# Talking-heads attention with a gated feed-forward network: the network's first product in float32 under the next batch's attention, x kept on chip, second head mixing on quarters of the array, 45 tiles a batch, w_out decoded late

## The chip, the cores and the metric

One core of a Trainium2 chip runs one program. The time is the device time of one execution in microseconds; the span of a profile runs from its first to its last instruction.

## The reference

For each of 4 batches: 12 heads, 448 rows, 64 elements a head. Scores are mixed over heads before and after the softmax; the result, 448 x 768, goes through a network with a convolution of three taps along the rows as its gate.

```python
scores = scale * q @ k^T                     # b h i j
scores = einsum('bhij,hg->bgij', scores, w_pre)
attn   = softmax(scores over j)              # sum + 1e-9
attn   = einsum('bhij,hg->bgij', attn, w_post)
x      = (attn @ v) as [b, 448, 768]
h      = relu(x @ w_in)                      # 768 -> 1024
gate   = sigmoid(conv_w[0]*h[i-1] + conv_w[1]*h[i] + conv_w[2]*h[i+1])
out    = (h * gate) @ w_out                  # 1024 -> 768
```

`w_in`, `conv_w` and `w_out` come as 64-bit floats and are decoded to float32 on the chip.

## The kernel before, in words

The rows of a batch are cut into four chunks of 120, 120, 120 and 100 query rows (`CHUNKS`, line 22), and a chunk into tiles of ten rows: 46 tiles a batch, 184 in all. A chunk goes through these steps, each a function:

- `qk` (line 372): scores of two heads (tile s), 64 x 64 quarters of the array; `qk_out` copies them, `relayout` (line 401) brings each head's scores by one DMA into a tile mt whose partitions hold ten rows of twelve heads.
- `premix` (line 411): two tiles at a time, mt times block-diagonal `wpre`, on quarters, into tiles m. `row_max`, `row_exp` (line 427), `sum_eps`, `sum_rec`, `post_w` make exponentials e and, for each tile, the second mixing's weights divided by the row sums (wn).
- `postmix` (line 451): for each tile four products, 124 partitions of e as weights, 112 columns of them, 120 columns of wn, on the whole array; the zeros of block-diagonal wn are multiplied too. `post_out` (line 462) copies the tile t on ScalarE.
- `av` (line 477): eight products a head pair on two halves of the array, into tile a of the pool ps_a (one buffer); `av_out` copies, `x_out` stores x (tensor xT) to DRAM.

A product of float32 operands appears as two records of TensorE in the trace (`postmix`: eight a tile).

The weights are decoded in 48 pieces of 256 KB (`dec_load`, `dec_step`, line 517 on): 24 of `w_in`, split into a high and a low part in reduced float32 (F32R), 24 of `w_out`, stored to DRAM. After all attention the network runs batch by batch: `x_load` and a split, `mm1` (line 625; three products of parts for each of six slices of 128, for each of eight slices f of the 1024), `relu`, `conv`, `gate`, `glu`, the split of g, and `mm2` (line 680) for 14 groups of 128 rows.

The order of instructions on each engine is planned ahead: `Order` (line 47) takes operations with a due time, an engine, a cost and the operations they wait for, and emits them in the order in which they could start. All DMAs of the main part are issued by SyncE (SP), in order, and each waits until the eighth DMA before it has landed; a DMA whose data is not ready holds those behind it.

Of the kernel before, what the change touches and what calls it, by code (L numbers as in the profile page):

```python
# [8 lines left out]
F32 = mybir.dt.float32  # L9
# [24 lines left out]

LAG = {"PE": P["lpe"], "DVE": P["ldve"], "ACT": P["lact"], "POOL": P["lpool"], "SP": P["lsp"]}

CUT = {"premix": 4, "qk": 4, "av": 2}
TURN = .093  # L40


RELAY = ("SP", (.82, .57))


class Order:

# [5 lines left out]
    def add(self, due, engine, cost, fn, *args, after=(), since=0.0):  # L53
        key = (fn.__name__, *args)
        assert key not in self.ops, key
        self.ops[key] = (due, len(self.ops), engine, cost, fn, args, tuple(after), since)

    def run(self, free, look):
        waits, users, ready = {}, {}, {e: [] for e in free}
        for key, op in self.ops.items():  # L60
            missing = {k for k in op[6] if k in self.ops}
            waits[key] = len(missing)
            for k in missing:
                users.setdefault(k, []).append(key)

        def release(key):
            due, i, engine, cost, fn, args, after, since = self.ops[key]
            t = since
            for k in after:
                if k in self.done:  # L70
                    end, e = self.done[k]
                    t = max(t, end + (LAG[e] if e != engine or e in ("SP", "DVE") else 0))
            ready[engine].append((due, i, t, key))
# [4 lines left out]
        left = len(self.ops)  # L78
        wire = 11.6
        cut = 1  # L80
        while left:
            best = None
            for e, ops in ready.items():
                if ops:
                    t0 = min(max(free[e], o[2]) for o in ops)
                    o = min(o for o in ops if o[2] <= max(t0, free[e]) + look)
# [6 lines left out]
            due, i, engine, cost, fn, args, after, since = self.ops[o[3]]  # L93
            if e == "PE":
                new = CUT.get(o[3][0], 1)
                if new != cut:
                    cost += TURN if new > 1 else 2 * TURN
                cut = new
            if isinstance(cost, tuple):
                cost, move = cost  # L100
                wire = max(wire, t + cost + .65) + move
                self.done[o[3]] = wire, "SP"
            else:
                self.done[o[3]] = t + cost, e
            free[e] = t + cost
            fn(*args)
            left -= 1
            for k in users.get(o[3], ()):
                waits[k] -= 1
                if waits[k] == 0:  # L110
                    release(k)


@with_exitstack
def tile_talking_heads_conv_glu(
# [13 lines left out]
    B, H, S, D = q.shape  # L129
    DM, FF = w_in.shape  # L130
    NP = H // 2
    NIB = S // 32
    JC = 4
    JW = S // JC
    scale = 1.0 / float(D) ** 0.5
    KC = DM // 128
    FC = FF // 128

    dram = ctx.enter_context(tc.tile_pool(name="dram", bufs=1, space=DRAM))

    xT = [dram.tile([128, NP * S], F32, name=f"xT{b}") for b in range(B)]

    w_out_s = dram.tile([FF, DM], F32, name="w_out_s")
# [18 lines left out]
    tasks = []  # L162

    def at(time, fn, *args):
        tasks.append((time, len(tasks), fn, args))

    def run(some):
        for _, _, fn, args in sorted(some, key=lambda e: (e[0], e[1])):
            fn(*args)

    if True:
        def pool(name, bufs, **kw):
            return ctx.enter_context(tc.tile_pool(name=name, bufs=bufs, **kw))

        const = pool("const", 1)
        ko_p = pool("ko", 7)
        qo_p = pool("qo", 2)
        nk_p = pool("nk", 2)
        nq_p = pool("nq", 1)
        wi_p = pool("wi", 1)  # L180
        mt_p = pool("mt", 2)
        st_p = pool("st", 3)
        e_p = pool("e", 4)
        sm_p = pool("sm", 4)
        wn_p = pool("wn", 3)
        at_p = pool("at", 2)
        v_p = pool("v", 6)
        x_p = pool("x", 2)
        dr_p = pool("dr", 3)
        dw_p = pool("dw", 2)  # L190
        ps_q = pool("ps_q", 2, space=PSUM)
        ps_m = pool("ps_m", 3, space=PSUM)
        ps_t = pool("ps_t", 2, space=PSUM)
        ps_a = pool("ps_a", 1, space=PSUM)

        wpre = const.tile([128, 2, 64], F32, name="wpre")
        wpost = const.tile([128, 12, HR, 2], F32, name="wpost")
        cws = const.tile([128, 3, FC], U32, name="cws")

        wraw = const.tile([128, 2, 12], F32, name="wraw")  # L200

        def load_weights():
            nc.gpsimd.memset(wraw, 0.0)
            nc.gpsimd.dma_start(out=wraw[4:124, 0, :],
                                in_=w_pre.rearrange("(o h) g -> o h g", o=1).to_broadcast([2 * HR, 12, 12]))
            for s in range(2):
                nc.gpsimd.dma_start(out=wraw[64 * s:64 * s + 12 * HR, 1, :],
                                    in_=w_post.rearrange("(o h) g -> o h g", o=1).to_broadcast([HR, 12, 12]))

        def emit_weights():  # L210
            raw = wraw
            pre = wpre[:, :, 0:12 * HR].rearrange("p s (r g) -> p s r g", g=12)
            bd = wn_p.tile([128, 2, HR, 12], F32, tag="wn", name="wbd")
            nc.gpsimd.memset(wpre, 0.0)
            for s in range(2):
                nc.vector.tensor_scalar(
                    out=bd[:, s],
                    in0=raw[:, 0, :].rearrange("p (o g) -> p o g", o=1).to_broadcast([128, HR, 12]),
                    scalar1=scale, scalar2=None, op0=ALU.mult)
                nc.gpsimd.affine_select(out=bd[:, s], in_=bd[:, s], pattern=[[-12, HR], [0, 12]],  # L220
                                        compare_op=ALU.is_ge, fill=0.0, base=-4 - 12 * HR * s, channel_multiplier=1)
                nc.gpsimd.affine_select(out=pre[:, s], in_=bd[:, s], pattern=[[12, HR], [0, 12]],
                                        compare_op=ALU.is_ge, fill=0.0, base=15 + 12 * HR * s, channel_multiplier=-1)
            bd2 = wn_p.tile([128, 12, HR, 2], F32, tag="wn", name="wbd2")
            nc.vector.tensor_copy(
                out=wpost.rearrange("p g r s -> p g (r s)"),
                in_=raw[:, 1, :].rearrange("p (g o) -> p g o", o=1).to_broadcast([128, 12, 2 * HR]))
            nc.gpsimd.affine_select(out=bd2, in_=wpost, pattern=[[0, 12], [-12, HR], [-64, 2]],
                                    compare_op=ALU.is_ge, fill=0.0, base=0, channel_multiplier=1)
            nc.gpsimd.affine_select(out=wpost, in_=bd2, pattern=[[0, 12], [12, HR], [64, 2]],  # L230
                                    compare_op=ALU.is_ge, fill=0.0, base=11, channel_multiplier=-1)

        cwraw = const.tile([128, 3 * FC, 2], U32, name="cwraw")
# [697 lines left out]
```

## Time and profile before

| | us |
|---|---|
| three runs | 734.51, 741.04, 742.68 |
| median | 741.04 |
| span of the profiled execution | 730.1 |
| TensorE busy | 691.4 |
| last exponential of the attention starts | 484.69 |

The profile gives the span of the execution it shows, and no device time of its own; the three runs lie 4.4 to 12.6 us above the span. Names of tiles: s scores, m first mixing, t second mixing, a values, h first product of the network, o its second. PE is TensorE, PEld its weight loads, DVE VectorE, ACT ScalarE, POOL GpSimd, SP SyncE. "64*64" in front of a shape is the rows and columns of the array in use.

### The profile page before, as it was taken

What the parts mean: (1) busy time and instruction counts of PE and PEld (TensorE: products, weight loads), DVE (VectorE), ACT (ScalarE), POOL (GpSimd) and SP (SyncE); (2) the same over time, 40 slices, a digit from 0 to 9 for tenths busy, and PEclk for the clock granted to TensorE, in tenths of its full rate; (3) what the DMA queues carried; (4) which work ended last, traced back from release to release, by engine and by line L of the source; (5) the groups of instructions that cost most, each with busy time, mean ns of one, the idle gap of its engine ahead of it and who ended that gap; (6) DMA issues with size and microseconds to landing.
All of it is one profiled execution on the core that took longest, in us unless ns stands there. A gap on an engine that the chain in (4) does not pass through costs nothing.

```text
span 730.1 us, 16150 instructions
## 1 busy us (share of the span) xinstructions
PE 691.4 (95%) x5804; PEld 525.2 (72%) x5804; DVE 419.0 (57%) x1150; ACT 398.5 (55%) x1011; POOL 98.8 (14%) x253
## 2 busy tenths in 40 slices
PE   4697989989999999999999999999999999999997
PEld 3244646656566666576666677788999999999997
DVE  3364576666687666566665654666825722842830
ACT  1255665867778657677767767773512421431420
POOL 7011212212122221121121100100000000000000
PEclk9888999999999999999999999999999999999999
DMA  6698876688876888967666833632212112110011
GB/s 106 198 163 189 210 187 166 201 212 198 196 211 167 222 217 228 217 183 213 198 173 200 204 116 93 198 107 63 51 44 60 38 44 70 27 52 38 1 40 48
DMA packets 104779, 101.26 MB, mean 139 GB/s; under 512 B 55848, under 2 KB 92028, under 8 KB 104700
## 3 DMA queue, kind: packets, MB, share of 16 engines
q1 hardware_dynamic: 102797, 99.62, 51.8%
q8 instruction: 46, 0.75, 0.5%
q10 hardware_dynamic: 1807, 0.61, 0.4%
q14 instruction: 33, 0.27, 0.1%
q0 software_dynamic: 96, 0.01, 0.0%
HBM read 46.48 MB, written 14.16 MB: 83 GB/s over the span
## 4 chain that ended last, share of the span: by engine, by line
PE 76%; DMA 14%; ACT 3%; DVE 2%; issue 2%; POOL 2%; SPq 1%; ACTq 0%; DVEq 0%; POOLq 0%
PE t L458 16%; PE h L637 16%; PE o L695 16%; PE s L385 9%; PE a L483 9%; PE m L419 8%; DMA mt<-st 7%; DMA raw<-in_moe_w_in_dram 5%; DMA nq<-in_q_dram 2%; ACT e L431 1%; POOL mt L313 1%; ACT st L338 1%; ACT at L466 1%; DVE nm L424 1%; DVE mq L301 1%
## 5 line engine op out<-in xcount | busy, mean ns | idle before, releaser
L458 PEld LDWEIGHTS t<-wn,e 124*112 124x112 f32 x1472 | 161.1, 180 | 61.9 <-PE s L385 19.0
L458 PE MATMUL t<-wn,e 124*112 124x120 f32 x1472 | 179.3, 276 | 3.0 <-ACT at L466 2.9
L338 ACT COPY st<-s 120x448 f32<-120x448 f32 (+1 forms) x180 | 94.0, 544 | 70.9 <-DMA mt<-st 39.6
L385 PE MATMUL s<-mk,mq 64*64 64x448 f32 (+2 forms) x768 | 117.2, 575 | 11.3 <-ACT st L338 8.5
L431 ACT ACTIVATE e<-m,nm 124x448 f32<-124x448 f32 x184 | 119.3, 649 | 10.7 <-DVE nm L424 6.9
L424 DVE TENSOR_REDUCE nm<-m 124x1 f32<-124x448 f32 x184 | 109.7, 613 | 25.0 <-PE m L419 22.2
L419 PE MATMUL m<-mt,wpre 64*64 64x448 f32 (+1 forms) x736 | 113.4, 566 | 8.7 <-ACT e L431 4.0
L466 ACT COPY at<-t 112x480 f32<-112x480 f32 x184 | 105.9, 575 | 26.0 <-PE t L458 25.3
L637 PE MATMUL h<-w,w 128*128 128x448 f32 x576 | 119.0, 367 | 0.0
L637 PEld LDWEIGHTS h<-w,w 128*128 128x128 f32 x576 | 107.8, 188 | 9.1
L695 PE MATMUL o<-wo,ga 128*128 128x384 f32 x504 | 91.9, 336 | 0.0
L695 PEld LDWEIGHTS o<-wo,ga 128*128 128x128 f32 x504 | 88.0, 188 | 0.1
L483 PEld LDWEIGHTS a<-at,v 112*64 112x64 f32 x1536 | 75.5, 137 | 15.8 <-ACT at L466 5.0
L437 POOL TENSOR_SCALAR sm<-sm 124x1 f32<-124x1 f32 x184 | 42.6, 231 | 319.5 <-ACT e L431 315.7
L483 PE MATMUL a<-at,v 112*64 112x120 f32 (+1 forms) x1536 | 83.5, 264 | 0.0
L442 DVE RECIPROCAL rs<-sm 124x1 f32<-124x1 f32 x184 | 29.1, 158 | 69.9 <-POOL sm L437 67.0
L419 PEld LDWEIGHTS m<-mt,wpre 64*64 64x64 f32 (+1 forms) x736 | 32.4, 135 | 49.7 <-ACT e L431 20.1
L641 ACT ACTIVATE hpad<-h 128x448 f32<-128x448 f32 x32 | 17.5, 547 | 90.6 <-PE h L637 71.8
L385 PEld LDWEIGHTS s<-mk,mq 64*64 64x64 f32 (+2 forms) x768 | 27.4, 129 | 48.1 <-ACT st L338 23.6
L448 DVE TENSOR_SCALAR wn<-wpost,rs 124x120 f32<-124x120 f32 x184 | 50.5, 274 | 10.7 <-PE t L458 4.6
L150 POOL TENSOR_SCALAR dw<-dw 128x256 f32<-128x256 f32 x48 | 41.5, 865 | 65.1 <-ACT dw L148 63.9
L706 DVE COPY os<-o 128x384 f32<-128x384 f32 x13 | 7.2, 558 | 71.4 <-PE o L695 71.4
(72 smaller groups left out, 519.4 us busy)
## 6 DMA issues: line engine op xcount, KB each, us to landing
mt<-st SPq DMA_DIRECT2D x144, 210.0 KB
nq<-in_q_dram SPq DMA_DIRECT2D x56, 168.0 KB
mt<-st SPq DMA_DIRECT2D x48, 175.0 KB
nk<-in_k_dram SPq DMA_DIRECT2D x72, 108.0 KB
raw<-in_moe_w_in_dram SPq DMA_DIRECT2D x24, 256.0 KB
raw<-in_moe_w_out_dram SPq DMA_DIRECT2D x24, 256.0 KB
v<-in_v_dram SPq DMA_DIRECT2D x48, 112.0 KB
out_dram<-os SPq DMA_DIRECT2D x13, 384.0 KB
```

The costliest lines, as they stand in the source:

```text
L338: nc.scalar.copy(out=out, in_=in_)
L385: nc.tensor.matmul(out=pqs[c, h - 1 + i][m:e], lhsT=qops[c][s, p, o + m:o + e], rhs=kops[b, p][s], start=True, stop=True)
L419: nc.tensor.matmul(out=pms[c, 2 * k + i][64 * s:64 * s + 64], lhsT=wpre[rows, i], rhs=mts[c][rows, 2 * k + s], start=True, stop=True)
L424: nc.vector.tensor_reduce(out=nm[0:PN], in_=pms[c, t][0:PN], axis=AX.X, op=ALU.max, negate=True)
L431: nc.scalar.activation(out=e[0:PN], in_=pms.pop((c, t))[0:PN], func=AF.Exp, bias=nm[0:PN], accum_out=sm[0:PN])
L437: nc.gpsimd.tensor_scalar(out=sm[0:PN], in0=sm[0:PN], scalar1=1e-9, scalar2=None, op0=ALU.add)
L448: nc.vector.tensor_scalar(out=wn[0:PN], in0=wpost.rearrange("p g r s -> p (g r s)")[0:PN], scalar1=rs[0:PN], scalar2=None, op0=ALU.mult)
L458: nc.tensor.matmul(out=ps[:, j].rearrange("p g r -> p (g r)"), lhsT=e[0:PN, j * JW:(j + 1) * JW], rhs=wn[0:PN], start=True, stop=True)
L466: nc.scalar.copy(out=ats[c][:, :, :, t * R:(t + 1) * R], in_=pts.pop((c, t)))
L483: nc.tensor.matmul(out=pas[c][64 * hh:64 * hh + 64, p % 3, 0:n], lhsT=vts[b, p][:, hh, j, :], rhs=ats[c][:, j, 2 * p + hh, 0:n], start=(j ...
L637: nc.tensor.matmul(out=ps, lhsT=w[:, sl], rhs=x, start=(kk == 0 and i == 0), stop=(kk == KC - 1 and i == 2))
L695: nc.tensor.matmul(out=ps[o], lhsT=g, rhs=w, start=(f == 0 and j == 0), stop=(f == FC - 1 and j == 2))
```

## The change

- The last chunk of a batch has nine tiles: 45 a batch; the odd tile's `premix` is one product on 124 partitions.
- `postmix` works on pairs of tiles. The weights wn lose the block of zeros (60 columns instead of 120); the two halves of e's partitions, and halves of 64 columns of e, go to the four quarters of the array. The results of a pair fill two banks, one for each five rows of every tile; `post_out` copies one on ScalarE and one on VectorE. Sums, reciprocals and `post_w` are done once a pair. v is padded to 512 rows with zeros.
- x of a batch stays in one tile on chip. `mm1` of batch b runs under the attention of batch b+1, in plain float32 without splits, with ps_a for its result; h goes to DRAM (`store_h`) and comes back in the last stage (`load_h`). Batch 3's `mm1` follows the attention.
- `w_in` is decoded into one tile, all 24 pieces by the first `mm1`; `w_out` from tile 106 on.
- The planner's costs and due times are new, and it models sixteen DMA rings and eight outstanding DMAs.

```diff
-CHUNKS = [(10, 12), (10, 12), (10, 12), (10, 10)]
+TILES = (12, 12, 12, 9)
...
+    turns = []
+    for c in range(NCH):
+        if c >= 4:
+            turns += [("mm1", c // 4 - 1, 2 * (c % 4) + i) for i in range(2)]
+        turns += [("av", c, 0), ("av", c, 3)]
...
+    for x, y in zip(order, order[1:]):
+        before[y] = ("relu", *x[1:]) if x[0] == "mm1" else ("av_out", *x[1:])
...
+            for i in range(len(some)):
+                add(n + 1 + P["po"] + .01 * i, "PE", .5, "postmix", *x, i, after=[("post_w", *x)] + (
+                    [("post_out", *prev, s) for s in range(2)] if prev else []))
...
+        ready = [("av_out", 4 * b + 3, p) for p in (0, 3)] + [("dec_step", i, 4) for i in range(N_IN)]
...
+            for kk in range(KC):
+                add(n + d * kk, "PE", .77, "mm1", b, f, kk, after=ready + turn + [("mm1", b, f, kk - 1)])
...
-            ps = ps_t.tile([JW, JC, 12, R], F32, tag="t", name="t")
-            for j in range(JC):
-                nc.tensor.matmul(out=ps[:, j].rearrange("p g r -> p (g r)"), lhsT=e[0:PN, j * JW:(j + 1) * JW],
-                                 rhs=wn[0:PN], start=True, stop=True)
+    if i == 0:
+        pts[c, k] = [ps_t.tile([128, 2, JC, 60], F32, tag="t", name="t") for s in range(2)]
+    e, wn = es.pop((c, 2 * k + i)), wns[c, k]
+    for j in range(JC):
+        for half in range(2):
+            o = min(128 * j + 64 * half, S - 64)
+            for s in range(2):
+                rows = slice(64 * s, 64 * s + 12 * HR)
+                nc.tensor.matmul(out=pts[c, k][s][64 * half:64 * half + 64, i, j], lhsT=e[rows, o:o + 64],
+                                 rhs=wn[rows, i], start=True, stop=True)
...
-            nc.scalar.copy(out=ats[c][:, :, :, t * R:(t + 1) * R], in_=pts.pop((c, t)))
+    copy_of(("ACT", "DVE")[s],
+            ats[c][:, :, :, o:o + 5 * n].rearrange("p j g (i r) -> p i (j g) r", r=HR),
+            pts[c, k][s][:, 0:n].rearrange("p i j (g r) -> p i (j g) r", r=HR))
...
-            for kk in range(k0, k1):
-                sl = slice(kk * 128, (kk + 1) * 128)
-                xh, xl = xp[b, kk]
-                for i, (w, x) in enumerate(((lo, xh), (hi, xh), (hi, xl))):
-                    nc.tensor.matmul(out=ps, lhsT=w[:, sl], rhs=x, start=(kk == 0 and i == 0),
-                                     stop=(kk == KC - 1 and i == 2))
+    if kk == 0:
+        pl, tag = (ps_a, "a") if b + 1 < B else (ps_q, "s")
+        phs[b, f] = pl.tile([128, S], F32, tag=tag, name="h")
+    nc.tensor.matmul(out=phs[b, f], lhsT=wi[:, kk, f * 128:(f + 1) * 128].bitcast(F32), rhs=xs[b][:, kk],
+                     start=(kk == 0), stop=(kk == KC - 1))
...
+def store_h(b, f):
+    nc.sync.dma_start(out=h_s[b][f * 128:(f + 1) * 128, :], in_=hss.pop((b, f)))
...
+def load_h(b, f):
+    nc.sync.dma_start(out=hpad[(FC * b + f) % 3][:, 1:S + 1], in_=h_s[b][f * 128:(f + 1) * 128, :])
```

TensorE in the attention of batch 1, before (s `qk`, m `premix`, t `postmix`, a `av`):

```order
L385 MATMUL s<-mk,mq 64x448 x2
L385 MATMUL s<-mk,mq 56x448 x2
L419 MATMUL m<-mt,wpre 64x448 x4
L458 MATMUL t<-wn,e 112x120 x8
L385 MATMUL s<-mk,mq 64x448 x2
L385 MATMUL s<-mk,mq 56x448 x2
L419 MATMUL m<-mt,wpre 64x448 x4
L483 MATMUL a<-at,v 64x100 x24
```

and in the attention of a later batch of the changed kernel (h is the first product of the batch before, six slices each):

```order
L709 MATMUL a<-at,v 64x120 x24
L624 MATMUL m<-mt,wpre 64x448 x4
L588 MATMUL s<-mk,mq 64x448 x2
L588 MATMUL s<-mk,mq 26x448 x2
L757 MATMUL h<-x,wi 128x448 x6
L668 MATMUL t<-wn,e 64x60 x32
L757 MATMUL h<-x,wi 128x448
L588 MATMUL s<-mk,mq 64x448 x2
L588 MATMUL s<-mk,mq 26x448 x2
L757 MATMUL h<-x,wi 128x448 x2
L624 MATMUL m<-mt,wpre 64x448 x4
L668 MATMUL t<-wn,e 64x60 x32
```

Twelve slices of the network's first product stand in each chunk from batch 1 on, in runs between scores, mixings and values.

SyncE late in batch 0, before (mt relayouts, raw pieces of weights, nk and nq loads of k and q, xT the store of x):

```order
L404 DMA mt<-st 10x10x448 x2
L517 DMA raw<-in_moe_w_in_dram 128x512
L293 DMA nq<-in_q_dram 32x6x224 x4
L507 DMA xT_57<-x 128x720
L404 DMA mt<-st 10x12x448 x4
L517 DMA raw<-in_moe_w_in_dram 128x512
L404 DMA mt<-st 10x12x448 x2
```

and late in batch 0 of the changed kernel:

```order
L738 DMA raw<-in_moe_w_in_dram 128x512
L604 DMA mt<-st 10x9x448
L547 DMA nk<-in_k_dram 32x864
L604 DMA mt<-st 10x9x448
L561 DMA nq<-in_q_dram 32x6x224
L738 DMA raw<-in_moe_w_in_dram 128x512
L604 DMA mt<-st 10x9x448
```

A piece of `w_in` stands after every second relayout or so. Its 24th piece stands behind 66 relayouts; before, 16 pieces and three stores of x stand ahead of the 66th.

## Rows read from the trace of the kernel before

**Rows 1.** The page: span, busy time of TensorE, chain that ended last by engine.

```profile
span 730.1 us, 16150 instructions
PE 691.4 (95%) x5804; PEld 525.2 (72%) x5804; DVE 419.0 (57%) x1150; ACT 398.5 (55%) x1011; POOL 98.8 (14%) x253
PE 76%; DMA 14%; ACT 3%; DVE 2%; issue 2%; POOL 2%; SPq 1%; ACTq 0%; DVEq 0%; POOLq 0%
```

**Rows 2.** Stages: from:to, length, busy of each engine, granted clock, DMA share, GB/s.

```profile
36.60:161.70 125.10, 112.91 (x1023) 70.07 (x1023) 80.22 (x252) 82.03 (x223) 22.58 (x61) 0.94 0.79 190
161.70:274.90 113.20, 109.85 (x1133) 72.01 (x1129) 78.10 (x245) 82.94 (x223) 25.30 (x62) 1.00 0.79 203
274.90:387.50 112.60, 109.36 (x1127) 72.92 (x1119) 70.91 (x217) 79.48 (x202) 22.40 (x60) 0.98 0.76 205
387.50:487.00 99.50, 99.02 (x1071) 70.74 (x1070) 59.03 (x186) 73.96 (x186) 14.04 (x50) 1.00 0.52 147
487.00:495.60 8.60, 8.60 (x122) 7.56 (x120) 4.53 (x9) 4.12 (x7) 0.00 (x0) 1.00 0.26 93
726.30:730.10 3.80, 0.00 (x1) 0.00 (x0) 0.56 (x1) 0.00 (x0) 0.00 (x0) 1.00 0.14 52
```

**Rows 3.** Stages, records of line 458 (`postmix`) on TensorE alone, batch 1.

```profile
161.70:274.90 113.20, 43.66 (x368) 1.00 0.79 203
```

**Rows 4.** Timeline of TensorE in batch 3: start, length, instructions.

```profile
442.86 0.97 PE L385 MATMUL s<-mk,mq 64*64 64x448 f32 x8
443.65 0.93 PE L419 MATMUL m<-mt,wpre 64*64 64x448 f32 x8
444.52 1.89 PE L458 MATMUL t<-wn,e 124*112 124x120 f32 x16
446.34 0.97 PE L385 MATMUL s<-mk,mq 64*64 64x448 f32 x8
...
447.99 2.68 PE L483 MATMUL a<-at,v 112*64 112x120 f32 x48
450.60 1.90 PE L458 MATMUL t<-wn,e 124*112 124x120 f32 x16
```

**Rows 5.** Groups by form: count, busy us, mean ns of one, idle before.

```profile
L466 ACT COPY at<-t 112x480 f32<-112x480 f32 x184 | 105.9, 575 | 26.0 <-PE t L458 25.3
L385 PEld LDWEIGHTS s<-mk,mq 64*64 64x64 f32 x384 | 27.2, 135 | 48.1 <-ACT st L338 23.6 <-issue 12.8 <-DVE st L340 4.1
L431 ACT ACTIVATE e<-m,nm 124x448 f32<-124x448 f32 x184 | 119.3, 649 | 10.7 <-DVE nm L424 6.9 <-DVE rs L442 3.4 <-POOL sm L437 0.4
L385 PEld LDWEIGHTS s<-mk,mq 64*36 64x36 f32 x96 | 4.2, 111 | 0.0
```

**Rows 6.** Timeline of weight loads around the same place.

```profile
442.86 0.19 PEld L385 LDWEIGHTS s<-mk,mq 64*64 64x64 f32 x8
```

**Rows 7.** DMA from batch 0's start to the 66th relayout's landing, 36.6 to 172.5.

```profile
DMA packets 24686, 25.74 MB, mean 189 GB/s; under 512 B 10648, under 2 KB 21084, under 8 KB 24668
q1 hardware_dynamic: 24668, 25.52, 77.5%
raw<-in_moe_w_in_dram SPq DMA_DIRECT2D x16, 256.0 KB
```

**Rows 8.** Chain of waits of batch 0, 36 to 165, by line.

```profile
by line: DMA raw<-in_moe_w_in_dram 24.9%; DMA mt<-st 13.5%; PE t L458 10.2%; DMA nq<-in_q_dram 8.2%; PE s L385 8.0%; PE m L419 7.0%; issue 5.3%; DVE nm L424 3.4%; DVE mq L301 3.2%; ACT e L431 2.9%; PE a L483 2.0%; ACT at L466 1.7%; SPq L293
```

**Rows 9.** The chain that ended last, its end: start, us, what.

```profile
495.62 26.23 PE h L637 x126
...
692.89 33.43 PE o L695 x192
```

**Rows 10.** Stages of the end (one batch of the network), as rows 2.

```profile
609.50:638.70 29.20, 29.20 (x146) 27.07 (x146) 19.55 (x38) 9.35 (x24) 0.00 (x0) 1.00 0.17 46
638.70:663.70 25.00, 25.00 (x145) 25.00 (x144) 9.11 (x19) 7.64 (x18) 0.00 (x0) 1.00 0.16 51
```

More of the change, by code (lines that the diff above doesn't have):

```diff
@@ L77, in run @@
                 release(key)
[L78 to L81, printed above, removed]
+        order = []
+        rings, landed = [0.0] * 16, [0.0] * QUEUES
+        shape = 1
+        for _ in range(len(ops)):
             best = None
[L83 to L86, printed above, removed]
+            for e, some in ready.items():
+                if some:
+                    t0 = min(max(free[e], o[2]) for o in some)
+                    o = min(o for o in some if o[2] <= max(t0, free[e]) + look)
                     t = max(free[e], o[2])
@@ new lines, in load_k0, with load_q0, keep_busy @@
+    def load_k0(p, eng):
+        for hh in range(2):
+            eng.dma_start(out=nat["k0"][:, p, :, D * hh:D * hh + D],
+                          in_=k[0, 2 * p + hh].rearrange("(c j) d -> j c d", c=JC))
+    def load_q0(c, g, eng=nc.sync):
+        s = slice(6 * g, 6 * g + 6)
+        _, i0, T = CHUNKS[c]
+        eng.dma_start(out=nat["q0"][0:R * T, c, s], in_=q[0, s, i0:i0 + R * T].rearrange("n i d -> i n d"))
+    def keep_busy(n):
+        ps = ps_q.tile([128, S], F32, tag="s", name="idle")
+        zero = nat["zero"]
+        for i in range(n):
+            nc.tensor.matmul(out=ps, lhsT=zero[:, 0:128], rhs=zero[:, 0:S], start=True, stop=True)
@@ new lines, in tile_talking_heads_conv_glu, with qk @@
+    pqs, sts = {}, {}
+    def qk(c, h):
+        b, i0, T = CHUNKS[c]
+        p, n = h // 2, R * T
+        o = q_rows(c)[2]
+        for i in range(2):
+            pqs[c, h - 1 + i] = ps_q.tile([128, S], F32, tag="s", name="s")
+        for m in (0, 64):
+            for i in range(2):
+                s = slice(64 * i, 64 * i + 64)
+                e = min(m + 64, n)
+                nc.tensor.matmul(out=pqs[c, h - 1 + i][m:e], lhsT=qops[c][s, p, o + m:o + e], rhs=kops[b, p][s],
+                                 start=True, stop=True)
@@ new lines, in tile_talking_heads_conv_glu, with premix @@
+    pms, es, sums, wns, pts, ats = {}, {}, {}, {}, {}, {}
+    PN = 64 + 12 * HR
+    def premix(c, k):
+        mt, some = nat["mt"][c % 2], PAIRS[c][k]
+        for t in some:
+            pms[c, t] = ps_m.tile([128, S], F32, tag="m", name="m")
+        if len(some) == 1:
+            t = some[0]
+            nc.tensor.matmul(out=pms[c, t][0:PN], lhsT=wpre[0:PN].rearrange("p s m -> p (s m)")[:, 0:PN],
+                             rhs=mt[0:PN, t], start=True, stop=True)
+            return
+        for s in range(2):
+            for i in range(2):
+                rows = slice(64 * i, 64 + 12 * HR * i)
+                nc.tensor.matmul(out=pms[c, some[i]][64 * s:64 * s + 64], lhsT=wpre[rows, i],
+                                 rhs=mt[rows, some[s]], start=True, stop=True)
@@ new lines, in tile_talking_heads_conv_glu @@
+    emit = {f.__name__: f for f in (
+        tr_k0, out_k0, load_q0, tr_q0, out_q0, load_k, tr_k, load_q, tr_q, qk, qk_out, relayout, premix, row_max,
+        row_exp, sum_eps, sum_rec, post_w, postmix, post_out, zero_v, load_v1, load_v, av, av_out, load_cw, emit_cw,
+        dec_load, dec_step, dec_store, mm1, relu, store_h, wo_load, wo_hi, wo_lo, net_init, room, load_h, conv, gate,
+        glu, g_hi, g_lo, mm2, mm2_out, store)}
+    with tc.manual_schedule():
+        load_weights()
+        prepare()
+        loads = [(load_q0, 0, 0), (load_q0, 0, 1)] + [(load_k0, p) for p in range(NP)]
+        for i, (fn, *a) in enumerate(loads):
+            fn(*a, nc.scalar if i in (1, 3) else nc.sync)
+        warm_up()
+        emit_weights()
+        keep_busy(P["busy0"])
+        for name, *a in plan(P)[0]:
+            emit[name](*a)
```

1215 lines of the change are left out of this document (566 added, 649 removed).

## The prediction

> **What bounds the kernel now.** I read the page first: TensorE is busy 691.4 of 730.1 us and holds 76% of the chain that ended last, DMA 14% [rows 1]. A TensorE that is busy everywhere says little by itself, since its ends are modelled, so the next view is the busy time by stage, cut where the first exponential of each batch starts [rows 2]. The reader is to see three regimes. Batch 0 takes 125.1 us, with a granted clock of 0.94 and TensorE idle for 12 us. Batches 1 and 2 take about 113 us with TensorE busy 97%. Batch 3 takes 99.5 us, because no scores of a next batch are made under it; its DMA share is 0.52 against 0.76 to 0.79 before. From 495.6 us TensorE is never idle: the network's products alone.
>
> The timeline of TensorE [rows 4] gives the price of a unit of work from start to start: scores of two heads (`qk`, tile s) 0.79 us; first mixing of two tiles (`premix`, m) 0.87 us up to the next start; second mixing of two tiles (`postmix`, t) 1.82 us; three head pairs of values (`av`, a) 2.61 us. So two tiles and their share of scores cost 3.48 us. A batch is 23 such steps, 80.0, one more `qk`, 0.8, eight `av` groups, 6 x 2.61 + 2 x 2.2 = 20.1, and about 2.2 for changes between full and divided array: 103.1 us. Batches 1 and 2 took 113.2 and 112.6, so some 10 us of each are waits. Batch 3 lacks nine `qk` (-7.1) and holds six products of the network (+1.2): 97.2 against 99.5, so 2.3 us of waits at the lower DMA share. That is TensorE-bound with a little DMA; 368 matmul records in batch 1 are 46 tiles of eight [rows 3].
>
> Batch 0 differs. The chain there lies 24.9% on loads of `w_in`, 13.5% on relayouts of scores and 8.2% on loads of q [rows 8]: 47% of 129 us. From its start to the landing of the 66th relayout, 135.9 us, DMA moved 25.74 MB at 189 GB/s with a share of 0.775 [rows 7].
>
> **The change part by part.** *Second mixing on quarters.* Per tile, 8 records of 120 columns on the whole array become 32 of 60 columns on four quarters, 8 per quarter one after the other. Before, a record takes 1.82/16 = 114 ns [rows 4]; with half the columns, 57 ns, and with four quarters side by side a tile is 8 x 57 = 0.46 us, two tiles 0.91, with 0.05 for the first weights 0.96. The weights must come at that pace too: eight weight loads of one `qk` end within 0.19 us, though one alone lasts 135 ns in the same form [rows 6, 5], so quarters load side by side. Bounds: below, 0.87 for two tiles (54 ns a record, half of `av`'s 2.61/24, since its 48 records of 120 columns run on two halves); above, no overlap at all, 64 records at `av`'s 2.61/48 = 54 ns, 3.5 us. I take 0.96, since `qk` and `premix` already run four quarters. The turn between `premix` (quarters) and `postmix` (whole) goes too: `premix` then costs 0.75 to 0.79; I take 0.77. A step becomes 0.79 + 0.77 + 0.96 = 2.52 us against 3.48.
>
> [...]
>
> *One bank for a pair of tiles in each of two halves.* `postmix` of a pair now waits for both copies (`post_out`) of the pair before, one on ScalarE, one on VectorE; a copy of this size took 575 ns [rows 5]. On TensorE 1.56 us of `qk` and `premix` lie between, so I cost it at nothing; uncovered it would be 0.3 us a pair. ScalarE loses 90 copies, VectorE gains them (some 13 us a batch).
>
> *45 tiles.* One tile and its chain less a batch: 22.5 steps.
>
> *First product in float32, under attention.* 18 records become 6 products of two passes. A pass of 448 columns is 0.79/2 = 0.39 us with its first weights [rows 4]; I take 0.375, so 0.75 a product, 48 x 0.75 = 36.0 us a batch, where 144 records at 26.23/126 = 0.208 us [rows 9] were 30.0. Bounds 0.42 (one pass would do) and 0.79. Three batches of it move from the end into batches 1 to 3, in four runs a chunk (order, below the diff), 16 x 0.28 = 4.5 us of turns a batch: a change of shape shows as 0.08 (`premix` 0.87 against `qk` 0.79 with as many columns [rows 4]); there and back, with the first weights of either side, I take 0.28. x stays on chip: 16 stores and 48 loads go, and the splits; 32 stores and 32 loads of h (224 KB) come, spread over 400 us.
>
> Batch 1, then: 22.5 x 2.52 = 56.7, 1.5 more `qk` 1.2, `av` 19.6 and turns 2.2, product 36.0 and turns 4.5: 120.2. Batch 2 the same, batch 3 113.1: 353.5. Waits: DMA carries about 18.6 MB in batch 1 against 23 before (no `w_in`, half of `w_out`, no x), over a longer time, near batch 3's share before, so 3 us a batch as there, 9; bounds 0 and 30 (10 a batch as batches 1 and 2 show).
>
> *Batch 0.* It has no product, so TensorE needs 2.52 x 24 + 6.3 (eight more `qk`) + 16 = 83 us to tile 48. But all 24 pieces of `w_in` must land before the first product. By the order, where the 24th is issued 66 relayouts are out; before, at the 66th, 16 were: eight more pieces (2.05 MB), less three x stores (1.1), a little more of k and v: 26.9 MB. At 189 GB/s that is 142 us; with the engines full, 189/0.775 = 244 GB/s, 110 us. I take the middle, 216 GB/s, 124.5 us: early relayouts no longer share with `w_in`, later ones share more. VectorE, 80.2 us busy there [rows 2], gains nine decodes and copies, loses splits: some 88 of 124.
>
> *End.* The last copies and values, 8.6 us before with 18 products in them (3.7), stay 5. Then batch 3's product, 36.0, and 14 row tiles at 33.43/4 = 8.36 [rows 9]: 117.0; last store 3.8 us after [rows 2]. The gates of batch 0 must be ready after those 36 us: VectorE needed 19.55 + 9.11 = 28.7 us a batch [rows 10], some 5 of it splits of x and copies out, plus 3 for `w_out`'s last parts: 27 against 36. So `w_out` late hides; if it doesn't, every us of it is on the end. Afterwards 23.7 against 29 a batch.
>
> Sum: 36.6 (start, same loads) + 124.5 + 353.5 less 5.2 (three tiles of batch 1 already in the first term) + 9 + 5 + 36 + 117 + 3.8 = 680.2 us of span. The page gives only a span; the three runs lie 4.4 to 12.6 above it, their median 10.9. With that the forecast is 691 us, 6.7% under 741.04. A measurement here tells about 1% from no change: 733.6 and 748.5 are the borders.
>
> **Rivals.** *A, DMA is not what holds batch 0* (its waits are latency of a queue in the wrong order): TensorE's 83 us decide, 41 less: 650. For it: a share of 0.775 is not full. Against: 47% of the chain is DMA. *B, the issue of records sets the pace on quarters*, at the 0.19/8 = 24 ns that rows show as an upper bound [rows 6]: 64 x 24 = 1.52 us instead of 0.96, 0.56 more in each of 66 steps outside batch 0, 37 us: 728. For it: so many records in so short a time occur nowhere before. Against: one load of the eight is 111 to 135 ns of those 0.19 us, so the starts lie far closer. [...] *C, slower:* `av` and the product share the one bank of pool ps_a. Each of 48 groups in batches 1 to 3 hands it over through a copy on VectorE or ScalarE, 0.6 us, behind an exponential (0.65) and a copy there, 1.5 to 2 us in all; if TensorE, which takes its rows in order, stands for 1.5 us at each, 72 us: 763. It makes the kernel slower from 1.2 us a hand-over. Against: the order puts a `postmix` of 0.96 us between most. *D, DMA stays at 189 GB/s and waits stay at 10 us a batch*: 17.5 + 21 more, 730; half of it is likely enough.
>
> **How the numbers follow.** Forecast 0.55 (668 to 714), A 0.13, B 0.07, C 0.06, D 0.19. The range reaches into A and D: 655 to 725. Faster by over 1%: the forecast, A, B and D without their dear ends, 0.90; within: those ends, 0.04; slower: C, 0.06.
>
> **What would show it.** t: 5,760 records, batches 1 to 3 with a step of some 2.5 us without product; starts of the exponentials: batch 1 near 155 us, 119 to 124 us a batch after; the products of the end from some 524 us without gaps. It is wrong if a step of two tiles takes 3 us or more on a TensorE that never waits, if TensorE waits for `av_out` or `relu`, if the w_in loads end before 140 us with TensorE idle, or if TensorE waits between 560 us and the end.

## The result and the profile after

The changed kernel takes 711.38 us (median of four runs, 709.99 to 713.12) beside 737.77 us for the kernel before on the same chip: a ratio of 0.965 with a 95% interval of 0.959 to 0.971. Forecast were 691 and a range of 655 to 725: faster, as said, but 20 us slower than the number. The profiled execution has a span of 708.4 us.

The page of the changed kernel: span, busy time, and the chain that ended last by engine and by line; the lines of before that answer to it are [rows 1].

```profile
span 708.4 us, 23470 instructions
PE 663.8 (94%) x9876; PEld 421.5 (59%) x9876; DVE 415.6 (59%) x976; ACT 343.8 (49%) x807; POOL 81.3 (11%) x185
PE 75%; DMA 14%; DVE 3%; ACT 3%; POOL 2%; issue 1%; SPq 1%; ACTq 0%; DVEq 0%; POOLq 0%
```

The stages (from:to, length, busy time and instructions of each engine, granted clock, DMA share, GB/s), cut as in [rows 2]: batches 0 to 3 at the starts of their first exponentials, the last copies, batch 3's first product, the second product, the last store.

```profile
38.90:162.50 123.60, 106.93 (x2118) 55.77 (x2112) 87.06 (x224) 72.10 (x178) 22.75 (x48) 0.94 0.80 189
162.50:289.30 126.80, 123.17 (x2232) 69.93 (x2232) 70.81 (x178) 70.89 (x173) 12.40 (x36) 1.00 0.65 169
289.30:416.70 127.40, 126.53 (x2306) 72.20 (x2301) 74.53 (x188) 72.56 (x179) 14.91 (x39) 1.00 0.61 167
416.70:540.90 124.20, 122.71 (x2216) 70.68 (x2212) 68.96 (x180) 68.56 (x168) 14.68 (x39) 1.00 0.43 129
540.90:551.40 10.50, 9.32 (x171) 6.42 (x160) 5.18 (x9) 3.71 (x7) 1.64 (x2) 1.00 0.43 138
551.40:587.20 35.80, 35.80 (x98) 18.18 (x97) 28.61 (x58) 16.34 (x28) 0.20 (x1) 1.00 0.44 134
587.20:704.40 117.20, 117.20 (x674) 116.89 (x672) 66.80 (x124) 31.43 (x60) 0.00 (x0) 1.00 0.27 88
704.40:708.40 4.00, 0.20 (x2) 0.00 (x0) 0.56 (x1) 0.00 (x0) 0.00 (x0) 0.97 0.16 60
```

Laid beside the sum of the forecast:

| term | forecast | measured | difference |
|---|---|---|---|
| start | 36.6 | 38.9 | +2.3 |
| batch 0 to tile 48 (at 168.5) | 124.5 | 129.6 | +5.1 |
| tile 48 to just behind the last exponential (540.9) | 357.3 | 372.4 | +15.1 |
| last copies and values | 5 | 10.5 | +5.5 |
| batch 3's first product | 36.0 | 35.8 | -0.2 |
| second product and last store | 120.8 | 121.2 | +0.4 |
| span | 680.2 | 708.4 | +28.2 |
| median less span | 10.9 | 3.0 | -7.9 |

The 2.3 us of the start were not looked into. The last exponential itself ends at 539.5. TensorE is idle for less than 4 us of each batch after batch 0, 6.0 us in all where 9 were forecast: the 15 us of the third row are no waits, they are work that costs more than its price. Where it lies shows in the timeline. TensorE at a step of an ordinary chunk of 120 rows (start, length, records):

```profile
400.57 1.16 PE L668 MATMUL t<-wn,e 60*64 60x60 f32 x64
401.55 0.94 PE L588 MATMUL s<-mk,mq 64*64 64x448 f32 x8
402.31 0.93 PE L624 MATMUL m<-mt,wpre 64*64 64x448 f32 x8
403.06 1.11 PE L668 MATMUL t<-wn,e 60*64 60x60 f32 x64
...
```

From start to start, t takes 0.98, s 0.76 and m 0.75 us, 2.49 a step where 2.52 was forecast. The same view while the scores of a chunk of 90 rows are made:

```profile
358.70 1.84 PE L588 MATMUL s<-mk,mq 64*64 64x448 f32 x8
360.47 0.98 PE L624 MATMUL m<-mt,wpre 64*64 64x448 f32 x8
361.27 1.11 PE L668 MATMUL t<-wn,e 60*64 60x60 f32 x64
362.20 1.79 PE L588 MATMUL s<-mk,mq 64*64 64x448 f32 x8
363.92 0.98 PE L624 MATMUL m<-mt,wpre 64*64 64x448 f32 x8
```

The same eight records of s take 1.77 and 1.72 us to the next start instead of 0.76, with no idle time in brackets behind them. The name "64*64" is that of the first record; four of the eight are 64 columns wide, and the other four only 26 (90 less 64). A batch has six such `qk`, each some 0.97 us longer, so 6 x 0.97 = 5.8 us a batch and some 17 us over batches 1 to 3.

The same view cut to 0.1 us inside the first `qk` keeps the two halves apart:

```profile
358.70 0.97 PE L588 MATMUL s<-mk,mq 64*64 64x448 f32 x4
359.60 0.94 PE L588 MATMUL s<-mk,mq 64*26 64x448 f32 x4
```

The four records of 26 columns start 0.90 us after those of 64, when these are almost through: the halves run one after the other. At a chunk of 120 rows the first records of both halves start together, four of them within 0.02 us from 401.55.

### The profile page after: what moved, and what is told of

Read it like the earlier page. It is cut to its first block, busy times and chain, and to the rows that moved or that the text cites. A ratio compares the mean times of both kernels' runs of the same rounds, so it can differ in the third digit from the quotient of the medians.

```text
span 708.4 us, 23470 instructions
## 1 busy us (share of the span) xinstructions
PE 663.8 (94%) x9876; PEld 421.5 (59%) x9876; DVE 415.6 (59%) x976; ACT 343.8 (49%) x807; POOL 81.3 (11%) x185
## 4 chain that ended last, share of the span: by engine, by line
PE 75%; DMA 14%; DVE 3%; ACT 3%; POOL 2%; issue 1%; SPq 1%; ACTq 0%; DVEq 0%; POOLq 0%
PE h L757 20%; PE o L851 16%; PE s L588 12%; PE a L709 9%; PE t L668 9%; DMA mt<-st 9%; PE m L624 8%; DMA nq<-in_q_dram 2%; DMA raw<-in_moe_w_in_dram 2%; POOL mt L492 1%; DVE nm L629 1%; DMA raw<-in_moe_w_out_dram 1%; ACT st L443 1%; DMA wo<-w_out_s 1%; ACT e L637 1%
## 5 line engine op out<-in xcount | busy, mean ns | idle before, releaser
L757 PE MATMUL h<-x,wi 128*128 128x448 f32 x384 | 156.9, 552 | 0.9 <-DVE x L717 0.9
L443 ACT COPY st<-s 120x448 f32<-120x448 f32 (+1 forms) x180 | 92.4, 533 | 103.6 <-DMA mt<-st 42.6
L668 PEld LDWEIGHTS t<-wn,e 60*64 60x64 f32 x5760 | 104.0, 136 | 53.7 <-issue 33.2
L668 PE MATMUL t<-wn,e 60*64 60x60 f32 x5760 | 110.7, 221 | 9.3 <-DVE wn L655 4.3
L851 PE MATMUL o<-wo,g 128*128 128x384 f32 x672 | 117.4, 337 | 0.0
L851 PEld LDWEIGHTS o<-wo,g 128*128 128x128 f32 x672 | 116.9, 188 | 0.4 <-DVE g L836 0.2
L757 PEld LDWEIGHTS h<-x,wi 128*128 128x128 f32 x384 | 69.3, 190 | 75.5 <-issue 63.1
L445 DVE COPY at<-t 128x480 f32<-128x480 f32 (+1 forms) x92 | 61.2, 665 | 55.3 <-PE t L668 55.1
L709 PEld LDWEIGHTS a<-at,v 128*64 128x64 f32 x1536 | 74.3, 137 | 20.8 <-issue 6.4
L709 PE MATMUL a<-at,v 128*64 128x120 f32 (+1 forms) x1536 | 83.6, 263 | 2.8 <-ACT at L443 1.6
L643 POOL TENSOR_SCALAR sm<-sm 124x2 f32<-124x2 f32 (+1 forms) x92 | 20.9, 227 | 372.4 <-ACT e L637 341.4
L443 ACT COPY at<-t 128x480 f32<-128x480 f32 (+1 forms) x92 | 57.6, 626 | 3.5 <-PE t L668 3.5
```

Of the source, the lines that this page charges most:

```text
L443: nc.scalar.copy(out=out, in_=in_)
L445: nc.vector.tensor_copy(out=out, in_=in_)
L668: nc.tensor.matmul(out=pts[c, k][s][64 * half:64 * half + 64, i, j], lhsT=e[rows, o:o + 64], rhs=wn[rows, i], start=True, stop=True)
L709: nc.tensor.matmul(out=pas[c][64 * hh:64 * hh + 64, p % 3, 0:n], lhsT=vts[b, p][:, hh, j, :], rhs=ats[c][:, j, 2 * p + hh, 0:n], start=(j ...
L757: nc.tensor.matmul(out=phs[b, f], lhsT=wi[:, kk, f * 128:(f + 1) * 128].bitcast(F32), rhs=xs[b][:, kk], start=(kk == 0), stop=(kk == KC - 1))
L851: nc.tensor.matmul(out=pos[r, o], lhsT=g, rhs=w, start=(f == 0 and j == 0), stop=(f == FC - 1 and j == 2))
```

## The experiments

All ratios are to the kernel before, run on the same chip. "e1" and so on are the first letters of the labels.

**e1 and e2: how wide the narrow half of a score is.** The second half of the columns of a 90-row chunk is taken 33 (e1) or 32 (e2) columns wide instead of 26; the added columns are zeros or the next head pair's, and nothing reads their results. The diff is e1's; e2 has 96 for 97.

```diff
+        w = n if n - 64 > 32 else 97
...
-                e = min(m + 64, n)
+                e = min(m + 64, w)
```

> Only the scores of the 90-row chunks change: the second half of their columns is 33 wide instead of 26, the seven more being columns that nobody reads. Theory (a half of 26 columns does not run beside the half of 64; the changed kernel's trace shows 1.72 us from such a qk to the next start, against 0.76 for the other chunks): each of the 24 qk of these chunks costs 0.76 us again, 0.97 us less each; 18 of them lie in batches 1 to 3 on a TensorE that hardly waits, so the batches go from 126.8, 127.4 and 124.2 us to some 121, 121.5 and 118, 17 us in all, and batch 0 gains 0 to 6: time 688 to 695. Rival (batches 1 to 3 are long because of waits and turns, and the 0.97 us would be waited for anyway): batches stay within 2 us, time 708 to 713.

Measured: 699.11 us, ratio 0.950 (0.946 to 0.953), and 12 us less than the changed kernel; that is 4 us above the theory's range. TensorE in e1, at the scores of a 90-row chunk:

```profile
353.00 1.11 PE L673 MATMUL t<-wn,e 60*64 60x60 f32 x64
353.93 0.94 PE L593 MATMUL s<-mk,mq 64*33 64x448 f32 x8
354.70 1.08 PE L629 MATMUL m<-mt,wpre 64*64 64x448 f32 x8
...
359.30 0.93 PE L593 MATMUL s<-mk,mq 64*64 64x448 f32 x8
360.06 0.93 PE L629 MATMUL m<-mt,wpre 64*64 64x448 f32 x8
```

Here s takes 0.77 and 0.76 us. The stages of batches 1 to 3:

```profile
162.40:282.80 120.40, 118.95 (x2236) 70.19 (x2236) 70.25 (x178) 70.31 (x174) 12.24 (x37) 1.00 0.68 176
282.80:408.00 125.20, 122.19 (x2306) 72.55 (x2298) 73.67 (x188) 72.39 (x180) 14.97 (x40) 1.00 0.63 170
408.00:525.50 117.50, 116.87 (x2212) 71.02 (x2204) 69.01 (x179) 68.23 (x168) 14.83 (x40) 1.00 0.45 137
```

Their sum is 363.1 us, where the changed kernel has 378.4 and the forecast had 353.5 + 9 = 362.5. Batches 1 and 3 gain 6.4 and 6.7 us. Batch 2 gains only 2.2: its records are busy for 4.3 us less, but TensorE idles 3.0 us instead of 0.9. Batch 0 gains nothing (124.6 us, below).

> As the run with 33 columns, but 32 wide. It tells where the border lies. If any second half narrower than 36 (the narrowest that the kernel before shows side by side) costs the 0.97 us, both 32 and 33 columns are slow; if 26 was slow for another reason than its width (its place at the end of the row block), both are fast. If 32 is slow (time about 711, qk of these chunks 1.7 us) and 33 is fast (some 691, 0.76 us), the border is between.

Measured: 710.16 us (one run), batches of 125.8, 127.9 and 122.9 us. TensorE in e2:

```profile
359.89 1.84 PE L593 MATMUL s<-mk,mq 64*64 64x448 f32 x8
361.66 0.98 PE L629 MATMUL m<-mt,wpre 64*64 64x448 f32 x8
```

With 32 columns a `qk` takes 1.77 us as with 26; with 33 it takes 0.77. So it isn't the number of columns that costs but a border between 32 and 33. At 26 columns the two halves run one after the other, 0.90 us apart in the changed kernel's trace above: 2 x 0.76 us, and some 0.2 is left over. Why they do is not shown.

**e3: no chunk of 90 rows.** Chunks of 12, 12, 11 and 10 tiles: the narrow halves are 46 and 36 columns wide, and the number of tiles stays 45.

```diff
-TILES = (12, 12, 12, 9)
+TILES = (12, 12, 11, 10)
```

> Chunks of 12, 12, 11 and 10 tiles instead of 12, 12, 12 and 9: still 45 tiles a batch and 23 pairs of which one is single, but no chunk has a second half narrower than 36 columns. Theory of the narrow half: 24 x 0.97 us less, of which 17 show, as with 33 columns: 688 to 697, a few us either way from the planner's order, whose due times were set for the other chunks. Rival: 706 to 716.

Measured: 702.33 us, ratio 0.952 (0.945 to 0.958), 5 us above the theory's range; e1 and e3 can't be told apart. It is another way round the same border, at another order of the instructions.

**e4: most loads of `w_in` left out.** 21 of 24 pieces are not loaded (the decodes work on what three loads left; the network's first product is not of the real weights).

```diff
+        if 3 <= i < N_IN:
+            raw = raws[i % 3]
+        else:
...
             nc.sync.dma_start(out=raw, in_=src[r * 128:(r + 1) * 128, o:o + CW].bitcast(U32))
```

> Leaves out the loads of 21 of the 24 pieces of w_in: those are decoded from the three that were loaded, so all work on the engines stays, and 5.4 MB of the 26.3 that DMA carries in batch 0 go. Theory (batch 0 waits for DMA at its 189 GB/s): batch 0 goes from 123.6 us towards 95 to 105, the span from 708 to some 682 to 690, and GB/s in batch 0 stays near 189. Rival (its waits are the latency of relayouts in SyncE's order, not bytes): batch 0 stays within 5 us of 123.6, and GB/s falls to some 150.

Measured: 698.44 us (one run); batch 0 takes 116.7 us instead of 123.6, at 163 GB/s: between the theory's range and the rival's. The 21 pieces are 5.5 MB, or 29 us at 189 GB/s; 7 came of it. Read alone, it says that bytes don't hold batch 0; e8 and e11 below say otherwise.

**e5: the quarters of the second mixing undone.** `postmix` on the whole array as before (wn of 120 columns with its zeros, e padded to 512 columns by a memset on GpSimd), all else as changed.

```diff
-            for half in range(2):
-                o = min(128 * j + 64 * half, S - 64)
-                for s in range(2):
-                    rows = slice(64 * s, 64 * s + 12 * HR)
-                    nc.tensor.matmul(out=pts[c, k][s][64 * half:64 * half + 64, i, j], lhsT=e[rows, o:o + 64],
-                                     rhs=wn[rows, i], start=True, stop=True)
+            nc.tensor.matmul(out=pts[c, k][i][:, j], lhsT=e[0:PN, 128 * j:128 * j + 128], rhs=wn[0:PN, i],
+                             start=True, stop=True)
```

> The changed kernel with the second mixing back on the whole array (weights 120 columns wide with zeros, e padded to 512 columns, four products of 120 columns a tile, a copy a tile); everything else as changed. Theory (the quarters give what the prediction put down, 3.48 us a step of two tiles on the whole array against 2.49 us measured now, and TensorE bounds the batches): about 0.97 us in each of the some 66 steps outside batch 0, 64 us, and up to 20 us more in batch 0: 775 to 795 us. Rival (something other than TensorE sets the length of the batches, so that the quarters give little): not above 740 us.

Measured: 759.54 us (one run), between the two ranges: without the quarters the other parts of the change make the kernel slower than before (735.67 there). By e1's price some 17 of these 24 us are the narrow halves, which e5 keeps. A step of TensorE in e5:

```profile
430.53 2.04 PE L670 MATMUL t<-wn,e 124*128 124x120 f32 x16
432.50 0.98 PE L593 MATMUL s<-mk,mq 64*64 64x448 f32 x8
433.30 0.93 PE L629 MATMUL m<-mt,wpre 64*64 64x448 f32 x8
434.16 2.04 PE L670 MATMUL t<-wn,e 124*128 124x120 f32 x16
```

t takes 1.97 us (1.82 before, at 112 columns of weights instead of 128 [rows 4]) and the step 3.63. The busy time of `postmix` alone in batches 1 to 3 (a stage's length, PE, PEld), of the changed kernel and of e5:

```profile
sum 378.40, PE 77.97 PEld 74.87; mean PE 25.99 PEld 24.96
```

```profile
sum 427.60, PE 134.71 PEld 125.15; mean PE 44.90 PEld 41.72
```

The quarters take 56.7 us out of TensorE's work there and 49.2 out of the three batches. The 49 us are below the 64 expected: only 56.7 us of work went, and in the changed kernel TensorE idles 6.0 us in these batches (the stages above), in e5 not at all. In batch 0 they give nothing: 122.9 us in e5, 123.6 changed. TensorE doesn't hold batch 0.

**e6: the slices of the first product in one run a chunk.** On top of e1, 24 changes of array shape fewer in batches 1 to 3.

```diff
-                d = .4
+                d = .05
```

> The kernel of e1 (second half of 33 columns) with the planner's distance between slices of the first product cut from 0.4 to 0.05, so that the slices of a chunk stand in one run and TensorE turns between array shapes 46, 38 and 40 times in batches 1 to 3 instead of 50, 48 and 50. Theory (a turn costs about 0.14 us each way): 24 turns fewer, 3 to 7 us under e1, 692 to 696 us. Rival (the turns are hidden, or the longer run lets ScalarE and the copies starve): 698 to 702 us.

Measured: 699.76 us, ratio 0.951 (0.946 to 0.957), the same as e1, the rival's side. What the fewer turns save doesn't reach the end; the forecast's 0.28 us for a turn there and back is neither borne out nor refuted by that.

**e7: `w_out` decoded earlier.** On top of e6.

```diff
-    dwo=5.652, wo0=109.872, look=0.047, step=2.1, busy0=8, k0a=-9.826, k0d=-0.06, m1=3.83, m1w=5.078, tail=4.129,
+    dwo=5.652, wo0=70.0, look=0.047, step=2.1, busy0=8, k0a=-9.826, k0d=-0.06, m1=3.83, m1w=5.078, tail=4.129,
```

> The kernel of e6 with the decoding of w_out planned from 70 instead of 109.9, so that its loads come earlier in the last batches. Theory (the 10.5 us between the last exponential and the last batch's product hold 2 to 4 us of ScalarE waiting for a w_out load, with the relu and the averaging behind it): 2 to 4 us under e6, with that stretch at 7 to 8.5 us. Rival (the loads then stand beside the relayouts of batches 1 and 2 and delay them): the same as e6 or slower, with longer batches 1 and 2.

Measured: 703.21 us, ratio 0.957 (0.953 to 0.962): not faster than e6. Batch 1 takes 127.5 us at a DMA share of 0.74 (e6: 120.8 at 0.69), as the rival says; batch 2 is no longer (126.1 against 127.8), and the stretch at the end takes 13.2 us instead of 11.1. So nothing speaks for an earlier decode, and the end isn't won that way. The chain of waits at the end of the changed kernel (start, us, what) passes through a load of `w_out`:

```profile
539.02 5.02 DMA wo<-w_out_s
...
544.06 0.03 ACT wo L777
...
546.24 0.45 ACT hs L762
```

SyncE issues this reload of the decoded `w_out` behind a store of h. ScalarE's cast waits for it, a `relu` of the first product waits behind the cast in ScalarE's order, and the bank of ps_a behind that. In e7 the same load stands in the chain with 4.58 us: what was moved is not what waits.

But the load is not why the stretch is long. TensorE is busy for 9.32 of its 10.50 us, and these are its only waits:

```profile
546.74 2.08 PE L709 MATMUL a<-at,v 128*64 128x90 f32 x48 [0.63 <-ACT hs L762]
549.37 2.08 PE L709 MATMUL a<-at,v 128*64 128x90 f32 x48 [0.55 <-DVE x L717]
```

So the 2 to 4 us that the theory hoped for weren't there to be won. What fills the stretch is work of the first product of batch 2 (its tile h alone, busy time of TensorE, its weight loads and ScalarE):

```profile
540.90:551.40 10.50, 4.32 (x11) 1.76 (x11) 0.54 (x1) 1.00 0.43 138
```

**e8: half of each relayout.** On top of e1; each relayout moves the first 224 of 448 columns, in as many transfers (the mixing of keys 224 to 447 is left out).

```diff
-        nc.sync.dma_start(out=nat["mt"][c % 2][4 + h:124:12, 0:T, :], in_=sts.pop((c, h))[0:R * T])
+        nc.sync.dma_start(out=nat["mt"][c % 2][4 + h:124:12, 0:T, 0:224], in_=sts.pop((c, h))[0:R * T, 0:224])
```

> The kernel of e1 with each relayout moving only the first 224 of 448 columns of a row (this leaves out the mixing of keys 224 to 447; the rest of the array is zero), the number of transfers and rows unchanged. Theory (the relayouts' bytes on the rings that they use bound batch 0, beside the w_in loads): batch 0 from 124.6 to 95 to 108 us. Rival (what bounds batch 0 is the order of issue, or the time from issue to landing whatever the size, or TensorE): batch 0 within 5 us of 124.6.

Measured: 668.67 us (one run), batch 0 105.8 us, the theory's side. Batch 0 in e1, as a stage:

```profile
37.80:162.40 124.60, 106.60 (x2117) 60.96 (x2111) 86.16 (x224) 72.65 (x178) 23.62 (x49) 0.90 0.84 190
```

and in e8:

```profile
36.30:142.10 105.80, 91.45 (x2116) 55.41 (x2110) 86.50 (x225) 71.51 (x178) 23.68 (x49) 0.98 0.74 180
```

As many records keep TensorE busy for 15 us less. The granted clock has a part in that. In batch 0 of the changed kernel it is 0.50 from 37.0 to 42.6 and from 90.5 to 100.5 us, and 1.00 from 42.7 to 90.3 and from 100.7 us on. At 0.50 eight records of s take 1.50 us to the next start and eight of m 1.49 (from 37.97 and 39.47 us); at 1.00 they take 0.76 and 0.75, as above. If the clock in e1 and e8 is made of the same two levels, its means of 0.90 over 124.6 us and of 0.98 over 105.8 are some 25 and 4 us at 0.50, by this estimate worth at most some 10 of the 15 us. In e1 the clock is lowest where TensorE idles most: 0.74 in the stages of 20 us from 78 and from 118 us, with 5.7 and 4.7 us idle. Of the chain of waits from 38 to 160 us, relayouts hold 40.6% in e1, 20.3% in e4 and 8.9% here. Both e4 and e8 move 19.0 MB in batch 0 (163 x 116.7 and 180 x 105.8), and yet differ by 11 us: bytes alone don't set its length.

**e9 and e10: is it the partitions that a relayout goes to, or its queue?** The mean DMA share of batch 0 in e1 is 0.84. A relayout goes into 10 partitions, and in batch 0 of the changed kernel, while only packets of relayouts (1792 bytes) are under way (5.9 us in all), there are most often ten at once (2.6 us). e9 lays the same rows into 15 or 30 partitions (this leaves the head mixing without meaning); e10 has `nc.gpsimd.dma_start` for `nc.sync.dma_start` in `relayout`. The diff is e9's.

```diff
+        w = T // 3
+        out = nat["mt"][c % 2][h:113 + h:8, 0:2 * w, :] if h < 8 else nat["mt"][c % 2][h - 8:117 + h - 8:4, 2 * w:T, :]
+        nc.sync.dma_start(out=out, in_=sts.pop((c, h))[0:R * T])
```

> The kernel of e1 with each relayout's rows laid into 15 or 30 partitions (8 or 4 rows each) instead of 10 (12 rows each): the same number of transfers, rows and bytes, and the same rows of 1792 bytes, but the scores of different heads no longer stand where the mixing wants them (this leaves the head mixing meaningless). [...] Rival (half the bytes helped as bytes, or as time from issue to landing that does not hang on the partitions): batch 0 within 4 us of 124.6, the whole 696 to 702.

Measured: 695.41 us (one run), batch 0 122.4 us at 190 GB/s and a share of 0.85, as e1. The rival's side: the partitions of the destination don't hold batch 0.

> The kernel of e1 with its relayouts issued by GpSimd's queue instead of SP's, nothing else. [...]

Measured: 707.8 us, ratio 0.962 (0.958 to 0.966), 9 us slower than e1; batch 0 takes 125.7 us and starts at 44.1 instead of 37.8. Another queue and a relieved SP (in e1 the issue of a relayout takes 0.79 us there, the median of 46) don't shorten batch 0; a gain that GpSimd's own waits hide (its relayouts stand 43.8 us there until ScalarE has copied the scores) isn't excluded.

**e11: half of the bytes of k and q.** On top of e1; their loads, after the first few, move half of the columns (the other half is left out), in as many transfers. The diff shows q's; k's are cut in the same way.

```diff
+        w = 224 if c == 2 else 112
...
-            out=nat["q", c].rearrange("p n r d -> p n (r d)")[o:o + 32, :, 0:224],
+            out=nat["q", c].rearrange("p n r d -> p n (r d)")[o:o + 32, :, 0:w],
...
-                :, :, 32 * dh:32 * dh + 224])
+                :, :, 32 * dh:32 * dh + w])
```

> The kernel of e1 with each load of k and q after the first few moving only half of its columns (this leaves out half of the k and q of batches 1 to 3; the rest of the tile keeps what was loaded first); the number of transfers and the issue on SP's queue unchanged. Some 3.5 MB of the 23.6 MB of batch 0 go, half of them before 98 us, where e4 took few bytes away. Theory (batch 0 is held by what DMA carries in its first half, whichever transfer it is; e8 took 4.7 MB of relayouts and gave 19 us): 13 us off batch 0, from 124.6 to 108 to 115. Rival (it is the relayouts' own way from issue to landing, which the chain names, that must be shorter): batch 0 from 118 to 124.6.

Measured: 682.3 us (one run), and batch 0 of e11:

```profile
38.40:152.80 114.40, 97.63 (x2127) 56.76 (x2121) 86.72 (x224) 71.83 (x178) 22.88 (x48) 0.94 0.73 183
```

2.7 MB fewer (190 x 124.6 less 183 x 114.4) give 10.2 us, 3.7 us a MB; e8's 4.6 MB gave 18.8, 4.1 a MB. So it isn't the relayouts' own length alone: k and q count as much. That is the theory's range, but not its reason, that the bytes of the first half count. The two halves of batch 0, cut where the 25th exponential starts, of e1 and of e11:

```profile
37.80:100.30 62.50, 52.93 (x1103) 31.45 (x1095) 40.26 (x102) 35.40 (x87) 8.51 (x23) 0.88 0.82 186
100.30:162.40 62.10, 53.67 (x1018) 29.51 (x1016) 45.90 (x123) 37.24 (x92) 15.11 (x26) 0.92 0.86 193
```

```profile
38.40:102.80 64.40, 53.08 (x1103) 29.87 (x1095) 40.63 (x102) 35.24 (x86) 8.04 (x23) 0.90 0.71 169
102.80:152.80 50.00, 44.55 (x1029) 26.90 (x1026) 46.09 (x123) 36.58 (x92) 14.85 (x25) 1.00 0.75 201
```

The first half gains nothing; all of the gain lies in the second, where the clock is higher too. e4 took 4.3 MB (189 x 123.6 less 163 x 116.7) and gave 6.9 against the changed kernel that it stands on, 1.6 a MB. Of the `w_in` pieces that batch 0 issues in e1, 6 lie before 98 us and 15 after, so e4 also took mostly late bytes, and late or early doesn't tell it from e11. One stage of e4 shows what stood in the way (share and GB/s stand last):

```profile
98.00:118.00 20.00, 19.93 (x358) 10.39 (x355) 15.72 (x40) 12.00 (x32) 5.12 (x10) 0.99 0.45 133
```

DMA has room there, and TensorE is full: three of the six narrow `qk` of batch 0 lie wholly in that stage, and e8 and e11, on top of e1, don't have their long time. How much of the distance between 1.6 and 4 us a MB is due to that, and how much to `w_in` being no transfer that the scores wait for, stays open; `w_in` was not thinned out on top of e1.

## Why the prediction was right or wrong

**Right: the mechanism and its unit prices.** The step of two tiles (2.49 us against 2.52), the first product (0.376 us a record, 35.8 a batch), the second (117.2 against 117.0) and the last store came in as worked out. With e5 the quarters are shown to be the change's gain: 49 us in batches 1 to 3, and without them the rest loses.

**Wrong step: every `qk` priced at 0.79.** That price was read at a chunk of 120 rows [rows 4], and at 100 rows before, whose narrow half is 36 wide [rows 5]. The change makes a chunk of 90 rows, and its narrow half is 26 wide. The order of the changed kernel showed it as `64x448 x2` and `26x448 x2`, and I priced both alike. Each of the 18 `qk` in batches 1 to 3 takes 1.72 to 1.77 us instead, some 17 us in all, more than the whole difference of 15.1 there. e1 takes it away and finds 363.1 us for the three batches against 362.5 forecast. The sum agrees, but partly by luck: TensorE idles 5.1 us there instead of 9, and some 4 us of the product's work fall behind the cut at the end, so the work that is left costs some 8 us more than its price; where, was not looked into. (The medians lie 12 us apart and not 15, since the execution of e1 that was profiled, 694.76 us, is the quickest of its four.)

**Wrong by half: the DMA rate of batch 0.** I took 216 GB/s, midway between the measured 189 and the 244 that I estimated for full engines from it and its share of 0.775. The trace of the changed kernel, from the start of batch 0 to the landing of the 24th `w_in` piece:

```profile
DMA packets 26206, 26.31 MB, mean 189 GB/s; under 512 B 12009, under 2 KB 22019, under 8 KB 26179
...
q1 hardware_dynamic: 26179, 25.95, 78.7%
raw<-in_moe_w_in_dram SPq DMA_DIRECT2D x24, 256.0 KB
```

It is 189 GB/s again at nearly the same share [rows 7], so these 26.31 MB (26.9 forecast) needed 139 us. That the term missed by 5.1 us only is luck, two errors against each other: I had tile 48 wait for the 24th piece, and it doesn't. Tile 48 starts at 168.5, and the first product at 182.3, after the last piece's decode. That DMA holds batch 0 is shown by e5 (a faster TensorE gives nothing), e8 and e11 (fewer bytes give 3.7 to 4.1 us a MB; a MB at the estimated 244 GB/s is 4.1). Whether it does so by its rate or by the time until relayouts, k and q land is open, and so is why the mean share stays near 0.8: e9 excludes the destination's partitions, and e10's other queue gave nothing.

**Mis-sized: the last copies, 5 against 10.5.** I carried over the 8.6 us of before less its products. The changed order leaves 4.3 us of batch 2's product there, which the forecast had in the batches before, and TensorE waits for 1.2 us; the 5 us that remain are as forecast.

**Mis-sized: the device time over the span, 10.9 against 3.0.** In each run here whose own execution was profiled the time lies 1.7 to 2.2 us over the span (710.16 and 708.4 in e2). The 10.9 held mostly that the execution profiled before was a quick one; it made up for 8 us of the other errors.

**The rivals.** A (TensorE alone decides batch 0, 650) is refuted by e5 and e11. B (24 ns a record at least) is refuted: 64 records of t in 0.98 us are 15 ns apart. C (the hand-over of the bank of ps_a) didn't come: TensorE idles 6.0 us in all over batches 1 to 3, where C had 72. D is half true, its rate and not its waits: 189 GB/s in batch 0, but some 2 us of idle TensorE a batch later, not 10.

## What to carry to other kernels

When a change alters a size, price each operation again at the new size, its narrowest piece too: 32 and 33 columns beside 64-wide quarters differ by 1.0 us a `qk` here, and padding with seven dead columns was worth 12 us of 711. A stretch that DMA holds is found by taking bytes out at the same number of transfers, for one kind of transfer at a time and all on the same kernel: here a MB was worth 1.6 to 4.1 us, and the lowest number came from a kernel in which TensorE filled part of the stretch. A faster TensorE gave nothing in the one batch that DMA holds; the bytes of relayouts, k and q there are the next thing to cut. And before a stretch is put down to a wait that stands in the chain, its busy time belongs beside it: at the end of this kernel the chain named a load, and TensorE was busy for 9.3 of 10.5 us.

## What was not expected of the hardware

The border between 32 and 33 columns: 1.77 against 0.77 us for the same eight records. And what shorter transfers gave shows up in TensorE's busy time too: in batch 0 some 2117 records were busy for 106.60 us at a granted clock of 0.90 in e1 and for 91.45 at 0.98 in e8, so a large part of the 18.8 us won there stands under "busy" and not under "idle".
